# An FNet and gated feed-forward layer on one core: VectorE's extra sums of the last quarter move from ahead of bank Y's drain to behind the sum that frees bank Z

## The chip, the cores and the metric

The kernel runs on one core of a Trainium2 chip. A core has TensorE (PE, matrix products into the banks of PSUM), VectorE (DVE), ScalarE (ACT), GpSimd (POOL) and SyncE (SP, which here issues all the DMAs). Each engine works through its own instructions in the order in which the program lists them and waits on semaphores where it needs another's result. The metric is the device time of one execution in microseconds (us); lower is better.

## The reference

The input is a sequence x of 2048 rows with 448 features in float32. Two sublayers follow each other, each with a layer norm in front and a residual around it:

```python
a = jnp.einsum("bsd,ed->bse", x, dft_hid_re)
b = jnp.einsum("bsd,ed->bse", x, dft_hid_im)
y = jnp.einsum("ts,bse->bte", dft_seq_re, a) - jnp.einsum("ts,bse->bte", dft_seq_im, b)
...
g = jnp.einsum("bsd,df->bsf", x, w_gate)
u = jnp.einsum("bsd,df->bsf", x, w_up)
h = _gelu(g) * u
return jnp.einsum("bsf,fd->bsd", h, w_down)
...
h = x + _A_ref(_layernorm(x, axis=-1), A_dft_seq_re, A_dft_seq_im, A_dft_hid_re, A_dft_hid_im)
h2 = h + _B_ref(_layernorm(h, axis=-1), B_w_gate, B_w_up, B_w_down)
```

The first sublayer is a Fourier mix over features and over the sequence; the second is a gated feed-forward block of width 1792.

## The kernel before

All products run in float16, but each float32 operand is split into a high part (its float16 value, made by ScalarE, line 105) and a low part (what is left, made by VectorE by subtracting the high part, line 109), and three partial products are added. On top of that the products are Strassen-like: sums and differences of blocks are formed first, so that seven block products do the work of eight.

The first half of the span does the Fourier mix and prepares the weights. The second half, which matters here, does the feed-forward block in four **quarters** of 512 rows (by pairs of 256), each of 14 **steps**; a step `t` (0 to 55) computes one block of 128 features of the hidden layer for the quarter's rows. The last quarter is steps 42 to 55. In a step TensorE uses three PSUM banks, X, Y and Z (`GateUp`, from line 1204). Its order in a step of the last three quarters is fixed by the loop from line 1427 on: `x_close`, `z_open` (the first products into Z), eight matmuls of the down projection (`dn_mm`), `y_mid`, ten more of `dn_mm`, `x_open` of the next step, `y_close`, `z_close`, three of `dn_mm`, `y_open` of the next step.

Between them three instructions of VectorE take the results out of the banks:

- the **first Z sum** in `y_mid` (line 1197, `hh<-pZ,u`): the hidden block from Z and from `u3`, ScalarE's copy of Y (line 1245). `z_close` adds more products into Z and so waits for it.
- **Y's drain** in `y_close` (line 1254, `hh<-pY,g`).
- the **second Z sum** in `z_close` (line 1197, `c<-pZ,u`). It frees bank Z: `z_open` of the next step waits for it.

The down projection works on 56 chunks; a chunk takes 128 columns of a quarter's hidden tile, and the blocks of one pair of steps. For each chunk `d` `dn_sums(d)` forms five sums of the hidden blocks (lines 1278 to 1280, into a tile `dn_s` of which there are three) and `dn_split(d)` makes the high and low parts (`dn_w`, or `dn_spare` where a tile no longer needed takes them): two instructions on ScalarE, two on VectorE. In each step `dn_ahead` has the sums of one chunk: GpSimd does the first two instructions, VectorE the last. Their split follows in the next step (the **ordinary split**).

The down projection runs 14 steps behind, so the last quarter's own chunks (numbers 42 to 55) have no step of the loop; TensorE multiplies them in a tail behind step 55. Some of them are therefore summed and split during the last quarter, as soon as their hidden blocks are complete: chunks 42 to 47 in steps 44, 46, 48, 50, 52 and 54, chunks 49 and 50 in steps 45 and 51. All three instructions of these **extra sums** are VectorE's. Their **extra split** follows at the end of the next step.

What stands where is a table `side`: `at(side, (t, k), work)` puts work at place `k` of step `t`, and `do(t, k)` in the loop issues it. Places 0 to 7 stand at given lines of the loop; places 2, 3 and 7 at the end of a step, in this order.

Of the kernel before, what the change touches and what calls it, by code (L numbers as in the profile page):

```python
# [32 lines left out]
def kernel(  # L33
# [38 lines left out]
    V, A, G, PE = nc.vector, nc.scalar, nc.gpsimd, nc.tensor  # L72
# [257 lines left out]
    def x_load(u, parts=(slice(0, 2),)):  # L330
        if parts[0].start == 0:
            t = pair_tile(f"x{u}")
            for g in range(2):
                xt[2 * u + g] = t[:, g, :], t[:, parts[0], :]
        for s in parts:
            src = x_pairs[u][:, s, :]
            t = xt[2 * u + s.start]
            nc.sync.dma_start(t[1] if s.start == 0 else t[0], src if s.start == 0 else src[:, 0, :])
# [9 lines left out]
    def x_stats(*tiles):  # L348
        n, tag = len(tiles), f"x{tiles[0]}"
        mv = norm_x[tiles] = small.tile([P, n, 2], F32, tag=f"mv{n}", name=f"mv_{tag}")  # L350
        sts = [small.tile([P, 6], F32, tag="st", name=f"st_x{i}") for i in tiles]
        for i, st in zip(tiles, sts):
            V.bn_stats(st, xt[i][0])
        for g, st in enumerate(sts):
            V.bn_aggr(mv[:, g, :], st)

    def x_root(*tiles):
        norm_x[tiles] = norm_x[tiles], root(norm_x[tiles], f"x{tiles[0]}")

    def x_rstd_steps(*tiles):  # L360
        mv, sd = norm_x.pop(tiles)
        found = []
        steps = rstd_steps(found, mv, sd, f"x{tiles[0]}")
        next(steps)
        for g, i in enumerate(tiles):
            norm_x[i] = mv, found[0], g
        yield
        yield from steps
# [354 lines left out]
    def at(t, n, *what):  # L723
        t.setdefault(n, []).extend(what)
# [21 lines left out]
    def chain(engine, costs, due, make, after=()):  # L746

        run, last = [], list(after)

        def step(first):  # L750
            if first:
                run.append(make())
            next(run[0])

        for k, cost in enumerate(costs):
            last = [add(engine, cost, due, lambda k=k: step(k == 0), after=last)]
        return last[0]
# [4 lines left out]
    def fixed(n, rank, engine, cost, what, after=(), lag=0.0):  # L762
        if n < FIRST:
            plan(n, rank, what)
            return None
        return add(engine, cost, T[n + 1], what, after=after, begin=T[n] - 1.0, lag=lag)
# [3 lines left out]
    for k, (i, i2) in enumerate(tiles_of):  # L770
        n = where["F", i]
        if k > 2:
            t = fixed(n - 10, 8, "SP", 0.1, lambda u=i // 2: x_load(u), lag=5.0)
            t = fixed(n - 7, 7, "V", 1.35, lambda i=i, j=i2: x_stats(i, j), [t])
            t = fixed(n - 6, 2, "A", 0.3, lambda i=i, j=i2: x_root(i, j), [t])
            if n - 6 < FIRST:
                fixed(n - 6, 5, "V", 0.6, lambda i=i, j=i2: x_rstd(i, j))
            else:
                t = chain("V", (0.2, 0.1, 0.1, 0.1), T[n - 5], lambda i=i, j=i2: x_rstd_steps(i, j), [t])
            t = fixed(n - 6, 5, "V", 0.15, lambda i=i, j=i2: x_bias(i, j), [t])  # L780
        for c in (i, i2):
            n = where["F", c]
# [6 lines left out]
        for c in (i, i2):  # L789
            n = where["F", c]  # L790
# [3 lines left out]
            if is_s(c // 2):  # L794
                t = drained = add("A", 1.05, T[n + 1] + 1.5, lambda i=c: feature_high(i), after=done + ring_w[-2:][:1] * (len(ring_w) > 1))
                t = chain("V", (0.56, 0.36, 0.36), T[n + 2], lambda i=c: feature_sums(i, V), [t])
                t = add("A", 1.45, T[n + 2] + 2.0, lambda i=c: sums_high(i), after=[t])
                t = add("V", 1.7, T[n + 2] + 3.5, lambda i=c: sums_low(i), after=[t])
                ring_w.append(t)
            else:  # L800
                t = add("A", 0.95, T[n + 1] + 1.0, lambda i=c: feature_high(i), after=done)
                t = drained = add("V", 1.07, T[n + 1] + 2.5, lambda i=c: feature_low(i), after=[t])
# [13 lines left out]
    for g, (p, u) in enumerate(units):  # L816
        n = where["U", p, u]
# [14 lines left out]
        if is_s(u):  # L832
            t = chain("V", (0.6, 0.34, 0.34), T[n] - 3.0, lambda p=p, u=u: seq_sums(p, u), [load] + sums_of)
# [11 lines left out]
    for p in range(N_PASS):  # L845
        q, j = divmod(p, 2)
        of_pass = [where["U", p, u] for u in range(N_UNIT)]
        n0, n = min(of_pass), max(of_pass) + 1
# [12 lines left out]
        t = add("A", 0.25, t0 + 14.0, lambda q=q, j=j: ffn_root(q, j), after=m)  # L861
        t = chain("V", (0.2, 0.1, 0.1, 0.1), t0 + 15.0, lambda q=q, j=j: ffn_rstd_steps(q, j), [t])
        last_e, h_done[p] = m, [store, t]
        if q < 2:
            t = add("V", 0.15, t0 + 16.0, lambda q=q, j=j: ffn_bias(q, j), after=[t])
            t = add("A", 1.35, t0 + 17.0, lambda q=q, j=j: ffn_norm_act(q, j, hp[q, j]), after=[t])
            h_done[p] = [store, t]
            for k in range(4):
                t = add("V", 0.36, t0 + 18.0 + k, lambda q=q, j=j, k=k: ffn_sums(q, j, (k,)), after=[t])
            for k in range(2):  # L870
                high = add("A", (0.65, 1.0)[k], t0 + 22.0 + k, lambda q=q, j=j, k=k: ffn_hi(q, j, (k,)), after=[t])
                t = high
            for k in range(5):
                t = add("V", (0.34, 0.87, 0.25, 0.35, 0.25)[k], t0 + 23.0 + k, lambda q=q, j=j, k=k: ffn_lo(q, j, (k,)), after=[t])
# [22 lines left out]
    for k, f in enumerate(order):  # L897
# [5 lines left out]
        t, lows = s2, []  # L903
        for m in range(4):
# [4 lines left out]
            t = high  # L909
# [7 lines left out]
    t = fixed(len(slots) - 14, 9, "SP", 0.1, lambda: down_load(0), last_e, lag=6.0)  # L917
# [349 lines left out]
    NC = NF // 2  # L1267
# [7 lines left out]
    def dn_sums(d, E=G):  # L1275
        t = dn_hid(d)
        s = dn_s[d] = fpool.tile([P, 5, P], F32, tag="dn_s", bufs=DN_S, name=f"dn_s{d}")
        E.tensor_add(s[:, 0:2], t[:, 0:2], t[:, 2:4])
        E.tensor_sub(s[:, 2:4], t[:, 1:4:2], t[:, 0:4:2])  # L1279
        V.tensor_add(s[:, 4], t[:, 0], t[:, 3])  # L1280
# [64 lines left out]
    side = {}  # L1345

    def do(t, k):
        for what in side.pop((t, k), ()):
            what()
# [24 lines left out]

    for n in range(6):
        t = 3 * NF + 2 * n + 2
        at(side, (t, 6), lambda n=n: dn_sums(6 * NC + n, V))
        at(side, (t + 1, 7), lambda n=n: dn_split(6 * NC + n, spare(n, 6 * NC + n) if n < 4 else None))
    for n, t in enumerate((3 * NF + 3, 3 * NF + 9)):
        at(side, (t, 6), lambda n=n: dn_sums(7 * NC + n, V))  # L1380
        at(side, (t + 1, 7), lambda n=n: dn_split(7 * NC + n, spare(4 + n, 7 * NC + n)))

    drains = {}
# [43 lines left out]
    for t in range(N_GU):  # L1427
        q, f = divmod(t, NF)
        if f == 0:
            if q == 1:  # L1430
                quarter0.close()
                odd_q = ctx.enter_context(tc.tile_pool(name="odd_q", bufs=1, side="right"))
            hh[q] = (fpool, odd_q)[q % 2].tile([P, NC, 4, TQ], F32, tag="hh", name=f"hh{q}")
            if 1 <= q <= 2:
                hops_tile(q + 1)
        ahead = {1: 5, 2: 6, 3: 7, 4: 8, 5: 9, 6: 10, 7: 11, 8: 12, 9: 13, 10: 14, 12: 15, 13: 16}.get(t) if t <= NF else t + 2
        if ahead and ahead < N_GU and ahead not in LATE:
            gw_load(ahead)
        d = t - NF
        if d >= 0 and d % NC == 1:  # L1440
            hr_load(d // NC)
        if t in (N_GU - 2, N_GU - 1):
            hr_load(t - N_GU + 8)
        nxt = GateUp(t + 1) if t + 1 < N_GU else None
        if q == 0:
            cur.x_close()
            nxt.x_open()
            if prev:
                prev.c_last()
            cur.y_mid()  # L1450
            late_prep(2 * t)
            if t > 0 and t % 2 == 0 and t < 2 * NC:
                down_hi(t // 2 - 1, 1)
            nxt.z_open()
            nxt.y_open()
            cur.y_close()
            cur.z_close()
            dn_ahead(t)
            if t > 0:
                down_prep(t - 1)  # L1460
            late_prep(2 * t + 1)
        else:
            do(t, 0)
            prev.c_last()
            cur.x_close()
            if t > NF:
                cur.z_open()
            if d + 1 < 6 * NC:
                dn_split(d + 1)
            dn_mm(d, range(0, 8))  # L1470
            cur.y_mid()
            dn_ahead(t)
            do(t, 6)
            dn_mm(d, range(8, 18))
            if nxt:
                nxt.x_open()
            do(t, 1)
            if not nxt:
                dn_mm(d, range(18, 21))
            do(t, 4)  # L1480
            cur.y_close()
            cur.z_close()
            if nxt:
                dn_mm(d, range(18, 21))
            do(t, 5)
            if nxt:
                nxt.y_open()
            if t == 2 * NC:
                down_hi(NC - 1, 1)
            if t == 2 * NC + 1:  # L1490
                down_lo(NC - 1, 1)
            do(t, 2)
            do(t, 3)
            do(t, 7)
        prev, cur = cur, nxt
    A6, A7 = 6 * NC, 7 * NC

# [105 lines left out]
```

## Time and profile before

| | |
|---|---|
| median of 3 runs | 712.17 us (712.1 to 712.65) |
| profiled execution | 712.42 us |
| its span | 710.6 us |
| TensorE busy | 701.3 us (99%) |
| VectorE busy | 544.6 us (77%) |
| ScalarE busy | 399.8 us (56%) |
| GpSimd busy | 197.1 us (28%) |
| granted TensorE clock | 1.0 |

The span is what lies between the first and the last instruction that the profile shows; the execution's time has what lies around it as well. The shares are means over the whole span: the last quarter, from about 590 to 679 us, has its own. In rows of the time line the first number is the start in us from the span's beginning, the second the duration of the group in us; matmuls overlap, so the distance from one group's start to the next tells more than the durations. `x6` is the number of instructions in a group. Buffer numbers are left out: `pZ` is bank Z of any step, `hh` the hidden layer, `hr` the residual rows.

### The profile page before, as it was taken

To read this page: it belongs to the slowest core of one execution; us is meant where nothing else is said; L and a number is where in the kernel's file an instruction comes from. 1 tells how busy PE (TensorE), PEld (TensorE's weight loads), DVE (VectorE), ACT (ScalarE), POOL (GpSimd) and SP (SyncE) were. 2 spreads that over 40 slices of the span, in tenths; PEclk is the share of its full clock that TensorE was granted. 3 is DMA by queue.
4 is the path that set the end of the run, shared out by engine and by line. 5 is a ranking of instruction groups with operands and counts; after the bars stand their busy time and mean duration, and the time that the engine had idled before them with its cause. 6 is when DMAs were issued, how large, how long until landed. Compare 5 with 4: busy or idle time off the path is not lost.

```text
span 710.6 us, 15025 instructions
## 1 busy us (share of the span) xinstructions
PE 701.3 (99%) x5902; PEld 570.6 (80%) x5902; DVE 544.6 (77%) x1131; ACT 399.8 (56%) x845; POOL 197.1 (28%) x225
## 2 busy tenths in 40 slices
PE   7999999999999999999999999999999999999998
PEld 4556567777776868686888889999999999998898
DVE  6799999899988987877368667575765755887876
ACT  5587574757656665645166665555555544454432
POOL 0000000000000000002026664474664745656442
PEclk9999999999999999999999999999999999999999
DMA  9366846799988697758267745847468574445301
GB/s 330 102 151 177 209 155 200 250 206 328 245 221 284 191 245 252 258 162 318 92 238 300 271 172 171 187 165 201 176 196 188 178 208 162 176 156 178 134 28 53
DMA packets 82935, 140.64 MB, mean 198 GB/s; under 512 B 41776, under 2 KB 60464, under 8 KB 82864
## 3 DMA queue, kind: packets, MB, share of 16 engines
q1 hardware_dynamic: 82864, 139.68, 63.8%
q8 instruction: 46, 0.75, 0.4%
q14 instruction: 25, 0.20, 0.1%
HBM read 110.17 MB, written 20.19 MB: 183 GB/s over the span
## 4 chain that ended last, share of the span: by engine, by line
PE 92%; DVE 3%; ACT 2%; issue 1%; DMA 1%; SPq 0%; DVEq 0%; ACTq 0%
PE acc L573 39%; PE acc_d L1132 15%; PE pY L1187 13%; PE pZ L1187 9%; PE ab L456 9%; PE pX L1187 8%; DMA wh_raw<-in_w_hid_dram 1%; DVE dn_w L109 1%; ACT dn_w L105 1%; DVE wh_lo L111 0%; DVE hh L1197 0%; ACT c L1262 0%; DVE dn_s L1280 0%; DVE dn_s L1279 0%; ACT u L1231 0%
## 5 line engine op out<-in xcount | busy, mean ns | idle before, releaser
L1187 PEld LDWEIGHTS <-gw 128*128 128x128 f16 x2184 | 213.3, 98 | 25.4 <-issue 3.0
L573 PE MATMUL acc<-b,ws 128*128 128x448 f16 (+1 forms) x1344 | 221.9, 312 | 0.0
L573 PEld LDWEIGHTS <-ws 128*128 128x128 f16 x1344 | 130.6, 98 | 70.7
L1187 PE MATMUL pY<-hops,gw 128*128 128x256 f16 x952 | 129.1, 273 | 0.0
L1132 PE MATMUL acc_d<-wd,dn_w 128*128 128x224 f16 x1050 | 122.3, 259 | 0.0
L234 POOL TENSOR_TENSOR wd_s<-wd 128x448 f32<-128x448 f32 x7 | 8.4, 1207 | 350.2 <-DMA wr<-in_w_seq_dram 331.7
L1132 PEld LDWEIGHTS <-dn_w 128*128 128x128 f16 x1050 | 101.2, 98 | 2.8
L105 ACT ACTIVATE ws<-wr 128x256 f16<-128x256 f32 (+2 forms) x96 | 63.1, 693 | 61.4 <-PE acc L573 43.5
L573 PE MATMUL acc<-b,wss 128*128 128x224 f16 x768 | 94.5, 259 | 0.0
L1187 PE MATMUL pZ<-hops,gw 128*128 128x256 f16 x616 | 85.5, 272 | 1.9 <-DVE c L1197 1.4
L1264 POOL TENSOR_TENSOR hh<-hh,c 128x256 f32<-128x256 f32 x56 | 45.6, 815 | 145.4 <-ACT c L1262 144.9
L1187 PE MATMUL pX<-hops,gw 128*128 128x256 f16 x616 | 83.3, 273 | 0.0
L111 DVE SCALAR_TENSOR_TENSOR ws<-wr,ws 128x256 f16<-128x256 f32 (+2 forms) x96 | 72.3, 781 | 9.1 <-ACT ws L105 9.0
L573 PEld LDWEIGHTS <-wss 128*128 128x128 f16 x768 | 73.8, 98 | 0.0
L109 DVE TENSOR_TENSOR dn_w<-hh,dn_w 128x256 f16<-128x256 f32 x50 | 25.7, 515 | 50.3 <-ACT dn_w L105 50.0
L456 PEld LDWEIGHTS <-xT 128*128 128x128 f16 x352 | 34.2, 98 | 32.5 <-issue 1.4
L109 DVE TENSOR_TENSOR dn_w<-dn_s,dn_w 128x640 f16<-128x640 f32 x50 | 54.9, 1098 | 7.0 <-ACT dn_w L105 5.9
L1231 ACT ACTIVATE u<-pY 128x256 f32<-128x256 f32 x56 | 21.4, 383 | 61.7 <-PE pY L1187 61.7
L1279 POOL TENSOR_TENSOR dn_s<-hh 128x256 f32<-128x256 f32 x42 | 52.8, 1258 | 0.0
L1226 ACT ACTIVATE pY<-pX 128x256 f32<-128x256 f32 x56 | 20.6, 368 | 50.0 <-PE pX L1187 50.0
L111 DVE SCALAR_TENSOR_TENSOR wss<-wsum,wss 128x1024 f16<-128x1024 f32 x32 | 39.3, 1229 | 9.8 <-ACT wss L105 9.8
L456 PE MATMUL ab<-wh_hi,xT 128*128 128x448 f16 x224 | 45.6, 352 | 0.5 <-DVE wh_hi L435 0.2
(120 smaller groups left out, 906.5 us busy)
## 6 DMA issues: line engine op xcount, KB each, us to landing
gw<-w_dram SPq DMA_DIRECT2D x54, 896.0 KB, 4.9
wr<-in_w_seq_dram SPq DMA_DIRECT2D x64, 512.0 KB, 4.6
gu_raw<-in_w_gu_dram SPq DMA_DIRECT2D x28, 384.0 KB, 4.4
w_dram<-gu_p SPq DMA_DIRECT2D x36, 256.0 KB, 3.0
hx<-in_x_dram SPq DMA_DIRECT2D x8, 448.0 KB, 6.3
h_dram<-hx SPq DMA_DIRECT2D x8, 448.0 KB, 5.3
hr<-h_dram SPq DMA_DIRECT2D x8, 448.0 KB, 5.4
x<-in_x_dram SPq DMA_DIRECT2D x7, 448.0 KB, 6.2
```

What stands on the lines that cost most here:

```text
L105: A.activation(dst, src, AF.Copy, scale=scale)
L109: V.tensor_sub(dst, src, hi)
L111: V.scalar_tensor_tensor(dst, src, scale, hi, op0=ALU.mult, op1=ALU.subtract)
L234: G.tensor_sub(s[:, 2:4], t[:, 0:2], t[:, 2:4])
L456: PE.matmul(feat[i][r][:, :D], xT[i][:, kx, :], w[:, kw, r * D : (r + 1) * D], start=n == 0, stop=n == 10,)
L573: PE.matmul(banks[k][:, cols], lhs, rhs, start=k not in begun, stop=stop, skip_group_check=True)
L1132: PE.matmul(acc[k // 2][:, k % 2 * HD : (k % 2 + 1) * HD], a_of(la, a), b_of(lb, b), start=first and m == 0 and k % 2 == 0, stop=last and ...
L1187: PE.matmul(ps, w[:, wl, wa + ws, :], ops[:, m + ms, :], start=first and n == 0, stop=last and n == len(terms) - 1, skip_group_check=True,)
L1226: A.activation(self.Y, self.X, AF.Copy)
L1231: A.activation(self.u2, self.Y, AF.Copy, scale=SC)
L1264: G.tensor_mul(c22, c22, self.c12)
L1279: E.tensor_sub(s[:, 2:4], t[:, 1:4:2], t[:, 0:4:2])
```

## The change

The extra sums get a place of their own, 8, which stands behind place 7 at the end of a step; place 6, between `y_mid` and `y_close`, goes away. Nothing else is changed. No instruction is added or taken away.

```diff
     for n in range(6):
         t = 3 * NF + 2 * n + 2
-        at(side, (t, 6), lambda n=n: dn_sums(6 * NC + n, V))
+        at(side, (t, 8), lambda n=n: dn_sums(6 * NC + n, V))
         at(side, (t + 1, 7), lambda n=n: dn_split(6 * NC + n, spare(n, 6 * NC + n) if n < 4 else None))
     for n, t in enumerate((3 * NF + 3, 3 * NF + 9)):
-        at(side, (t, 6), lambda n=n: dn_sums(7 * NC + n, V))
+        at(side, (t, 8), lambda n=n: dn_sums(7 * NC + n, V))
         at(side, (t + 1, 7), lambda n=n: dn_split(7 * NC + n, spare(4 + n, 7 * NC + n)))
...
             cur.y_mid()
             dn_ahead(t)
-            do(t, 6)
             dn_mm(d, range(8, 18))
...
             do(t, 7)
+            do(t, 8)
         prev, cur = cur, nxt
```

VectorE in step 44, before, from the ordinary chunk's last sum to the first row of step 45 (`dn_s42` are the extra sums, `pY_44` and `pZ_44` the banks of this step, `dn_w32` the ordinary split):

```order
L1280 TENSOR_TENSOR dn_s32_8173<-hh2_6627 128x128
L1278 TENSOR_TENSOR dn_s42_8177<-hh3_7947 128x256
L1279 TENSOR_TENSOR dn_s42_8177<-hh3_7947 128x256
L1280 TENSOR_TENSOR dn_s42_8177<-hh3_7947 128x128
L1254 SCALAR_TENSOR_TENSOR hh3_7947<-pY_44_8105,g1_44_8142 128x256
L1197 SCALAR_TENSOR_TENSOR c12_44_8211<-pZ_44_8144,u2_44_8129 128x256
L109 TENSOR_TENSOR dn_w32_8244<-hh2_6627,dn_w32_8244 128x256
```

And with the change:

```order
L1280 TENSOR_TENSOR dn_s32_8173<-hh2_6627 128x128
L1254 SCALAR_TENSOR_TENSOR hh3_7947<-pY_44_8105,g1_44_8142 128x256
L1197 SCALAR_TENSOR_TENSOR c12_44_8207<-pZ_44_8144,u2_44_8129 128x256
L1278 TENSOR_TENSOR dn_s42_8222<-hh3_7947 128x256
L1279 TENSOR_TENSOR dn_s42_8222<-hh3_7947 128x256
L1280 TENSOR_TENSOR dn_s42_8222<-hh3_7947 128x128
L109 TENSOR_TENSOR dn_w32_8244<-hh2_6627,dn_w32_8244 128x256
```

The extra sums stand behind the second Z sum (`c12_44`) and directly ahead of the ordinary split. No extra split stands in step 44.

VectorE from the first Z sum of step 45 to that of step 46, before (`dn_s49` are the extra sums of step 45, `dn_spare` the extra split of chunk 42, `dn_w33` the ordinary split):

```order
L1197 SCALAR_TENSOR_TENSOR hh3_7947<-pZ_45_8237,u3_45_8263 128x256
L1280 TENSOR_TENSOR dn_s33_8266<-hh2_6627 128x128
L1278 TENSOR_TENSOR dn_s49_8270<-hh3_7947 128x256
L1279 TENSOR_TENSOR dn_s49_8270<-hh3_7947 128x256
L1280 TENSOR_TENSOR dn_s49_8270<-hh3_7947 128x128
L1254 SCALAR_TENSOR_TENSOR hh3_7947<-pY_45_8198,g1_45_8235 128x256
L1197 SCALAR_TENSOR_TENSOR c12_45_8304<-pZ_45_8237,u2_45_8222 128x256
L109 TENSOR_TENSOR dn_spare_8320<-hh3_7947,dn_spare_8320 128x256
L109 TENSOR_TENSOR dn_spare_8320<-dn_s42_8177,dn_spare_8320 128x640
L109 TENSOR_TENSOR dn_w33_8343<-hh2_6627,dn_w33_8343 128x256
L109 TENSOR_TENSOR dn_w33_8343<-dn_s33_8266,dn_w33_8343 128x640
L1197 SCALAR_TENSOR_TENSOR hh3_7947<-pZ_46_8336,u3_46_8362 128x256
```

And with the change:

```order
L1197 SCALAR_TENSOR_TENSOR hh3_7947<-pZ_45_8237,u3_45_8263 128x256
L1280 TENSOR_TENSOR dn_s33_8266<-hh2_6627 128x128
L1254 SCALAR_TENSOR_TENSOR hh3_7947<-pY_45_8194,g1_45_8235 128x256
L1197 SCALAR_TENSOR_TENSOR c12_45_8300<-pZ_45_8237,u2_45_8218 128x256
L109 TENSOR_TENSOR dn_spare_8316<-hh3_7947,dn_spare_8316 128x256
L109 TENSOR_TENSOR dn_spare_8316<-dn_s42_8222,dn_spare_8316 128x640
L1278 TENSOR_TENSOR dn_s49_8321<-hh3_7947 128x256
L1279 TENSOR_TENSOR dn_s49_8321<-hh3_7947 128x256
L1280 TENSOR_TENSOR dn_s49_8321<-hh3_7947 128x128
L109 TENSOR_TENSOR dn_w33_8343<-hh2_6627,dn_w33_8343 128x256
L109 TENSOR_TENSOR dn_w33_8343<-dn_s33_8266,dn_w33_8343 128x640
L1197 SCALAR_TENSOR_TENSOR hh3_7947<-pZ_46_8336,u3_46_8362 128x256
```

Y's drain and the second Z sum now come directly behind the ordinary sum; the extra sums stand behind the extra split of chunk 42 and ahead of the ordinary split, which is followed by the first Z sum of step 46.

VectorE in step 52 and the start of step 53, before (`dn_s46` are the extra sums, `dn_w50` the extra split, `dn_w40` the ordinary one):

```order
L1197 SCALAR_TENSOR_TENSOR hh3_7947<-pZ_52_8912,u3_52_8938 128x256
L1280 TENSOR_TENSOR dn_s40_8941<-hh2_6627 128x128
L1278 TENSOR_TENSOR dn_s46_8945<-hh3_7947 128x256
L1279 TENSOR_TENSOR dn_s46_8945<-hh3_7947 128x256
L1280 TENSOR_TENSOR dn_s46_8945<-hh3_7947 128x128
L1254 SCALAR_TENSOR_TENSOR hh3_7947<-pY_52_8868,g1_52_8910 128x256
L1197 SCALAR_TENSOR_TENSOR c12_52_8979<-pZ_52_8912,u2_52_8892 128x256
L109 TENSOR_TENSOR dn_w50_8995<-hh3_7947,dn_w50_8995 128x256
L109 TENSOR_TENSOR dn_w50_8995<-dn_s50_8847,dn_w50_8995 128x640
L109 TENSOR_TENSOR dn_w40_9018<-hh2_6627,dn_w40_9018 128x256
L109 TENSOR_TENSOR dn_w40_9018<-dn_s40_8941,dn_w40_9018 128x640
```

And with the change:

```order
L1197 SCALAR_TENSOR_TENSOR hh3_7947<-pZ_52_8912,u3_52_8938 128x256
L1280 TENSOR_TENSOR dn_s40_8941<-hh2_6627 128x128
L1254 SCALAR_TENSOR_TENSOR hh3_7947<-pY_52_8864,g1_52_8910 128x256
L1197 SCALAR_TENSOR_TENSOR c12_52_8975<-pZ_52_8912,u2_52_8888 128x256
L109 TENSOR_TENSOR dn_w50_8991<-hh3_7947,dn_w50_8991 128x256
L109 TENSOR_TENSOR dn_w50_8991<-dn_s50_8897,dn_w50_8991 128x640
L1278 TENSOR_TENSOR dn_s46_8996<-hh3_7947 128x256
L1279 TENSOR_TENSOR dn_s46_8996<-hh3_7947 128x256
L1280 TENSOR_TENSOR dn_s46_8996<-hh3_7947 128x128
L109 TENSOR_TENSOR dn_w40_9018<-hh2_6627,dn_w40_9018 128x256
L109 TENSOR_TENSOR dn_w40_9018<-dn_s40_8941,dn_w40_9018 128x640
```

Here too the extra sums stand between the extra split and the ordinary one.

## The prediction

> **What bounds the kernel now.** I read the page's busy shares first, then the view of who waited for whom, then the time line of the last quarter, which nearly all rows below are from (start, duration, engine, line, operation; in brackets the idle time ahead and who ended it).
>
> ```profile
> PE 701.3 (99%) x5902; PEld 570.6 (80%) x5902; DVE 544.6 (77%) x1131; ACT 399.8 (56%) x845; POOL 197.1 (28%) x225
> PE pZ L1187 <- DVE c L1197: 1.4, 2, 0.7
> ```
>
> TensorE is the bound: any microsecond that is won or lost must show as TensorE waiting or no longer waiting. In all of the span it waits twice for VectorE's second Z sum, `c<-pZ`. How much such waits cost is read from the distance of repeating work, because the ends of matmuls are modelled. In a step, the six matmuls that open the next step's bank X are the mark:
>
> ```profile
> 606.63 0.82 PE L1187 MATMUL pX<-hops,gw 128*128 128x256 f16 x6
> 612.90 0.82 PE L1187 MATMUL pX<-hops,gw 128*128 128x256 f16 x6
> 619.17 0.82 PE L1187 MATMUL pX<-hops,gw 128*128 128x256 f16 x6
> 619.82 0.71 PE L1187 MATMUL pY<-hops,gw 128*128 128x256 f16 x5
> 620.48 0.71 PE L1187 MATMUL pZ<-hops,gw 128*128 128x256 f16 x5
> 625.55 0.82 PE L1187 MATMUL pX<-hops,gw 128*128 128x256 f16 x6
> 644.58 0.82 PE L1187 MATMUL pX<-hops,gw 128*128 128x256 f16 x6
> 648.77 0.82 PE L1187 MATMUL pZ<-hops,gw 128*128 128x256 f16 x6 [0.68 <-DVE c L1197]
> 651.80 0.82 PE L1187 MATMUL pX<-hops,gw 128*128 128x256 f16 x6
> 662.26 0.82 PE L1187 MATMUL pZ<-hops,gw 128*128 128x256 f16 x6 [0.68 <-DVE c L1197]
> 671.56 0.82 PE L1187 MATMUL pX<-hops,gw 128*128 128x256 f16 x6
> ```
>
> The mark at 606.63 stands in step 44, the one at 671.56 in step 54. An undisturbed step takes 612.90 - 606.63 = 6.27. Ten steps from 606.63 to 671.56 take 64.93, so 2.23 us are lost in them. 651.80 - 644.58 = 7.22 is one step with a Z wait: 0.95 too long. The other (at 662.26) has the same idle time, so two of them make 1.90, and the remaining 0.33 is three steps like the one from 619.17 to 625.55, which is 0.11 too long. There the loss is at `z_close`: from 619.82 to 620.48 five matmuls take 0.66, while six of the same shape take 0.65 just before (619.17 to 619.82), so five should take 0.54. I put the same 0.11 inside each 0.95 (`z_close` of steps 50 and 52), which leaves 0.84 for each Z wait. So 1.68 is all that this change can win by freeing bank Z earlier.
>
> **What sits around the place where the sums go.** This is VectorE with its neighbours from the end of step 45 to the middle of step 46:
>
> ```profile
> 615.35 0.41 DVE L1197 SCALAR_TENSOR_TENSOR c<-pZ,u 128x256 f32<-128x256 f32 x1
> 615.79 0.38 ACT L1231 ACTIVATE u<-pY 128x256 f32<-128x256 f32 x1 [1.67 <-PE pY L1187]
> 616.37 0.73 ACT L105 ACTIVATE dn_spare<-dn_s 128x640 f16<-128x640 f32 x1
> 617.13 0.83 DVE L109 TENSOR_TENSOR dn_spare<-dn_s,dn_spare 128x640 f16<-128x640 f32 x1 [0.20 <-ACT dn_spare L105]
> 617.48 1.07 POOL L1264 TENSOR_TENSOR hh<-hh,c 128x256 f32<-128x256 f32 x1 [2.88 <-ACT c L1262]
> 618.02 0.81 DVE L109 TENSOR_TENSOR dn_w<-hh,dn_w 128x256 f16<-128x256 f32 x1
> 618.50 0.38 ACT L1245 ACTIVATE u<-pY 128x256 f32<-128x256 f32 x1
> 618.50 0.91 POOL L1278 TENSOR_TENSOR dn_s<-hh 128x256 f32<-128x256 f32 x1
> 618.75 1.34 DVE L109 TENSOR_TENSOR dn_w<-dn_s,dn_w 128x640 f16<-128x640 f32 x1
> 619.38 1.31 POOL L1279 TENSOR_TENSOR dn_s<-hh 128x256 f32<-128x256 f32 x1
> 620.02 0.41 DVE L1197 SCALAR_TENSOR_TENSOR hh<-pZ,u 128x256 f32<-128x256 f32 x1
> ```
>
> The first Z sum (620.02) had its operand from ScalarE at 618.50 + 0.38 = 618.88, but starts 1.14 later, because VectorE is still in the splits. Its end, 620.43, releases `z_close` at 620.48. So here the low parts of two splits form a chain with no slack: `y_open` of step 46, ScalarE's `u` (615.79), its two high parts, the extra split's low part (617.13 to 617.96), the ordinary split's two low parts, the first Z sum, `z_close`.
>
> **The change part by part.** It moves eight groups of three VectorE instructions (steps 44, 45, 46, 48, 50, 51, 52, 54). It adds and removes none, and no DMA moves; ScalarE, GpSimd and SyncE keep their orders.
>
> *Steps 44, 48, 50, 54: no extra split stands behind the second Z sum.* There the moved sums meet slack:
>
> ```profile
> 609.08 0.41 DVE L1197 SCALAR_TENSOR_TENSOR c<-pZ,u 128x256 f32<-128x256 f32 x1
> 610.84 0.45 DVE L109 TENSOR_TENSOR dn_w<-hh,dn_w 128x256 f16<-128x256 f32 x1 [1.36 <-ACT dn_w L105]
> 637.10 0.47 DVE L109 TENSOR_TENSOR dn_w<-hh,dn_w 128x256 f16<-128x256 f32 x1 [0.45 <-ACT dn_w L105]
> 649.77 0.48 DVE L109 TENSOR_TENSOR dn_w<-hh,dn_w 128x256 f16<-128x256 f32 x1 [1.06 <-ACT dn_w L105]
> 677.55 0.43 DVE L1197 SCALAR_TENSOR_TENSOR hh<-pZ,u 128x256 f32<-128x256 f32 x1 [3.62 <-ACT u L1245]
> ```
>
> In step 44 VectorE idles 1.36 behind the second Z sum, and that sum itself comes earlier once the sums no longer stand ahead of it. In step 48 the same work only changes its place ahead of 637.10, where 0.45 of idle is left; in step 50 1.06 are left behind the sums (649.77), in step 54 3.62. Cost nothing, cover VectorE's wait for ScalarE's high part; without it they would cost at least 0.87 each (below). In step 50 the 0.84 Z wait goes.
>
> *Steps 45, 46, 51, 52: the sums go behind an extra split and ahead of the ordinary one.* By the order of rows they stand between 617.13's instruction and 618.02's. They can't use VectorE's idle time before 617.13, which is a wait of the split ahead of them. Behind them queue the two low parts and the first Z sum, and for this waits `z_close`. In step 52 the other 0.84 goes too. So at `z_close` of steps 46, 47, 52 and 53 the delay grows by X, the time by which the first Z sum is later. What X is, the trace bounds:
>
> ```profile
> 646.06 1.50 POOL L1123 TENSOR_TENSOR hr<-hr,v 128x224 f32<-128x224 f32 x2
> 646.17 0.88 DVE L1278 TENSOR_TENSOR dn_s<-hh 128x256 f32<-128x256 f32 x1
> 646.97 0.88 DVE L1279 TENSOR_TENSOR dn_s<-hh 128x256 f32<-128x256 f32 x1
> 647.97 0.41 DVE L1254 SCALAR_TENSOR_TENSOR hh<-pY,g 128x256 f32<-128x256 f32 x1
> 672.21 0.41 DVE L1278 TENSOR_TENSOR dn_s<-hh 128x256 f32<-128x256 f32 x1
> 673.08 0.41 DVE L1254 SCALAR_TENSOR_TENSOR hh<-pY,g 128x256 f32<-128x256 f32 x1
> 656.39 1.06 POOL L1264 TENSOR_TENSOR hh<-hh,c 128x256 f32<-128x256 f32 x1 [2.82 <-ACT c L1262]
> 657.41 0.90 POOL L1278 TENSOR_TENSOR dn_s<-hh 128x256 f32<-128x256 f32 x1
> 658.28 1.31 POOL L1279 TENSOR_TENSOR dn_s<-hh 128x256 f32<-128x256 f32 x1
> 659.54 1.51 POOL L1123 TENSOR_TENSOR hr<-hr,v 128x224 f32<-128x224 f32 x2
> ```
>
> Alone the three sums take 673.08 - 672.21 = 0.87; beside GpSimd 647.97 - 646.17 = 1.80, where one sum takes 0.88 instead of 0.41: each meeting with a GpSimd instruction costs 0.47. The same is seen at 618.02 (0.81, against 0.45 at 610.84: 0.36 more) and 618.75 (1.34 against 0.83: 0.51 more). Those are two meetings, with GpSimd instructions two and three of a queue of three (617.48, 618.50, 619.38). With the sums in front, the same three GpSimd instructions meet the three sums instead, and the low parts behind them run free: three meetings in place of two. X = 0.87 + 1 x 0.47 = 1.34. Around step 52's start GpSimd has five (656.39 to 659.54, the last row being two), and five VectorE instructions to meet: five in place of two, X = 0.87 + 3 x 0.47 = 2.28. Lower end: no more meetings than before, X = 0.87. Upper end: the sums pay the full 1.80 and the low parts still pay theirs; in the five-deep place 2.28 stays. I take the count of meetings, since it explains each of the rows above.
>
> That the meetings exclude each other is also what the Trainium skill says in "SBUF — State Buffer", section "SBUF: two separate sides": VectorE instructions with two SBUF inputs and GpSimd share a port pair, which one of them holds for a whole instruction while the other blocks, and which isn't a split of bandwidth. The trace agrees (0.88 against 0.41). By that rule the count of meetings decides and the sum is the +4.73 below; if the two instead shared the bandwidth for as long as both have work, the sums would pay their 1.80 everywhere, and the sum would be that of rival C, +6.11.
>
> *The sum.* Won: 2 x 0.84 = 1.68. Lost: 1.34 + 1.34 + 2.28 + 1.34 = 6.30. At `z_close` of step 53 the 0.11 appears anew, which the Z wait had hidden. The other 0.11 stay. -1.68 + 6.30 + 0.11 = +4.73. The tail behind step 55 is TensorE's own, by the last row of the chain that ended last:
>
> ```profile
> 679.37 28.19 PE acc_d L1132 x294
> ```
>
> It only starts later. The profiled span of 710.6 becomes 715.3, its execution 712.42 becomes 717.15; the median shown, 712.17, becomes 716.9.
>
> **The rivals.**
>
> *A. Not slower: the sums keep GpSimd out.* Between 617.96 and 620.02 the low parts need 2.06, of which 0.36 + 0.51 = 0.87 is waiting for GpSimd (that the sums alone also take 0.87 is chance). If five VectorE instructions back to back let GpSimd in only afterwards, the three sums fill exactly those 0.87: X is about 0, and only the win is left, 710.6. It decides if X is below (1.68 - 0.11)/4 = 0.39. For it: 617.13 ran its full 0.83 while GpSimd's 617.48 stretched to 1.07. Against it: at 646.17 and 646.97, back to back, GpSimd got in between.
>
> *B. No extra meeting.* X = 0.87 four times: -1.57 + 3.48 = +1.91, 714.1. For it: GpSimd's third instruction may slip behind the low parts, as 619.38 does now behind 618.75. Against it: it would then meet those, which is a meeting too.
>
> *C. Full price.* 3 x 1.80 + 2.28 - 1.57 = +6.11, 718.3. For it: 1.80 is measured for these very instructions. Against it: only three GpSimd instructions are queued there.
>
> *D. The change doesn't do what it says*, since the two orders keep the same work behind the same waits: then 712.2. Against it: the order shows the sums behind `c<-pZ` in all eight steps.
>
> **How the numbers follow.** Forecast 716.9 with a chance of 0.70, A 0.05, B 0.10, C 0.13, D 0.02. The range 714.1 to 718.3 goes from B to C, the ends of the unknown X. A measurement of this kernel tells about 0.2% (1.4 us) from no change. Slower by more: the forecast, C and nearly all of B, 0.91. Within: D and a part of B in which one of the four places is hidden, 0.05. Faster: A, less a part that lands near no change, 0.04.
>
> **What would show it.** In the changed kernel the waits of `pZ` for `c` are gone, and in their place stand four of `pZ` for `hh L1197`, shown at some 1.2 to 2.3 us each (the one at step 52's `z_close` the longest). The sums in steps 45, 46, 51, 52 last 0.8 to 0.9 and the low parts behind them come down to about 0.45 and 0.83, save in step 52. Steps 44, 48, 50 and 54 are 6.27 to 6.4 long. It would be wrong if the first Z sum in step 46 starts within 0.4 of where it starts now (A), or if GpSimd's queue there is deeper than three.

## The result, and the profile after

The changed kernel takes 717.35 us (median, 717.24 to 718.83), the kernel before 712.19 beside it: 1.0076 times as long, 95% interval 1.0062 to 1.009. A second group of executions, beside 712.34 us of the kernel before, gave 717.8 us and 1.0075 (1.0062 to 1.0087).

In the view of who waited for whom (us in total, times, longest) the row of `pZ` waiting for `c` is gone, and the row of `pZ` waiting for `hh` has grown. Before, it was a single wait of 0.3 us in an earlier quarter (at 425.73), which is still there:

```profile
PE pZ L1187 <- DVE hh L1197: 6.5, 5, 2.3
```

TensorE's time line of the last quarter (start, duration, engine, line, operation) shows the other four of these waits, at `z_close` of steps 46, 47, 52 and 53, and the two marks that answer to 606.63 and 671.56 before:

```profile
606.66 0.82 PE L1187 MATMUL pX<-hops,gw 128*128 128x256 f16 x6
...
619.85 0.71 PE L1187 MATMUL pY<-hops,gw 128*128 128x256 f16 x5
621.92 0.71 PE L1187 MATMUL pZ<-hops,gw 128*128 128x256 f16 x5 [1.36 <-DVE hh L1197]
...
626.98 0.82 PE L1187 MATMUL pX<-hops,gw 128*128 128x256 f16 x6
...
629.70 0.71 PE L1187 MATMUL pZ<-hops,gw 128*128 128x256 f16 x5 [1.36 <-DVE hh L1197]
...
660.73 0.71 PE L1187 MATMUL pY<-hops,gw 128*128 128x256 f16 x5
663.71 1.23 PE L1187 MATMUL pZ<-hops,gw 128*128 128x256 f16 x5 [2.27 <-DVE hh L1197]
...
670.31 0.82 PE L1187 MATMUL pX<-hops,gw 128*128 128x256 f16 x6
670.97 0.71 PE L1187 MATMUL pY<-hops,gw 128*128 128x256 f16 x5
672.91 0.70 PE L1187 MATMUL pZ<-hops,gw 128*128 128x256 f16 x5 [1.24 <-DVE hh L1197]
...
677.98 0.82 PE L1187 MATMUL pX<-hops,gw 128*128 128x256 f16 x6
```

The ten steps take 71.32, so 8.62 us are lost in them, where 2.23 were before. At `z_close` of step 46 the distance 619.85 to 621.92 is 2.07 in place of 0.55, so 1.52 are lost; in step 47 it is 1.52 again, in step 52 2.43, in step 53 1.39. With the two old 0.11 that makes 7.08. The remaining 1.54 come from something else: the five matmuls at 663.71 last 1.23 in place of 0.71, and from there to the next mark it is 6.60, against 5.06 behind the wait in step 46 (621.92 to 626.98). TensorE ran at a lower clock there; this execution took 718.83 us, and the others, at a mean clock of 1.0, took 717.24 to 717.36 with spans of 715.5 to 715.6. So the change itself costs about 5 us, and this one execution 1.5 more.

VectorE and GpSimd from the extra split of step 45 to the first Z sum of step 46, with the change:

```profile
617.16 0.82 DVE L109 TENSOR_TENSOR dn_spare<-dn_s,dn_spare 128x640 f16<-128x640 f32 x1 [0.20 <-ACT dn_spare L105]
617.90 0.95 DVE L1278 TENSOR_TENSOR dn_s<-hh 128x256 f32<-128x256 f32 x1
618.78 0.94 DVE L1279 TENSOR_TENSOR dn_s<-hh 128x256 f32<-128x256 f32 x1
619.65 0.81 DVE L1280 TENSOR_TENSOR dn_s<-hh 128x128 f32<-128x128 f32 x1
620.38 0.41 DVE L109 TENSOR_TENSOR dn_w<-hh,dn_w 128x256 f16<-128x256 f32 x1
620.72 0.81 DVE L109 TENSOR_TENSOR dn_w<-dn_s,dn_w 128x640 f16<-128x640 f32 x1
621.45 0.41 DVE L1197 SCALAR_TENSOR_TENSOR hh<-pZ,u 128x256 f32<-128x256 f32 x1
```

```profile
617.51 1.06 POOL L1264 TENSOR_TENSOR hh<-hh,c 128x256 f32<-128x256 f32 x1 [3.06 <-ACT c L1262]
618.54 0.90 POOL L1278 TENSOR_TENSOR dn_s<-hh 128x256 f32<-128x256 f32 x1
619.40 0.91 POOL L1279 TENSOR_TENSOR dn_s<-hh 128x256 f32<-128x256 f32 x1
```

The two engines take turns: each of the three sums waits for one GpSimd instruction and lasts about 0.53 longer (0.95 for 0.41 alone). Then GpSimd's queue is empty, and the low parts behind run at 0.41 and 0.81, where they took 0.81 and 1.34 before. The first Z sum starts at 621.45, where it started at 620.02; with the 0.03 by which all of this trace is later (606.66 against 606.63) it is 1.40 late.

Around the start of step 52, where GpSimd has five instructions, the sums meet the first three in the same way (0.95, 0.94 and 0.81), and the low parts behind them meet the last two, at 0.88 and 1.27 in place of a bare 0.41 and 0.81:

```profile
661.15 1.50 POOL L1123 TENSOR_TENSOR hr<-hr,v 128x224 f32<-128x224 f32 x2
661.26 0.88 DVE L109 TENSOR_TENSOR dn_w<-hh,dn_w 128x256 f16<-128x256 f32 x1
662.05 1.27 DVE L109 TENSOR_TENSOR dn_w<-dn_s,dn_w 128x640 f16<-128x640 f32 x1
663.25 0.41 DVE L1197 SCALAR_TENSOR_TENSOR hh<-pZ,u 128x256 f32<-128x256 f32 x1
```

### The profile page after: what moved, and what is told of

Its sections match the earlier page's. It is cut to its first block, busy times and chain, and to the rows that moved or that the text cites. A ratio compares the mean times of both kernels' runs of the same rounds, so it can differ in the third digit from the quotient of the medians.

```text
span 717.1 us, 15024 instructions
## 1 busy us (share of the span) xinstructions
PE 702.7 (98%) x5902; PEld 571.3 (80%) x5902; DVE 542.9 (76%) x1131; ACT 399.3 (56%) x845; POOL 194.7 (27%) x225
## 4 chain that ended last, share of the span: by engine, by line
PE 91%; DVE 4%; ACT 2%; issue 1%; DMA 1%; SPq 0%; DVEq 0%; ACTq 0%
PE acc L573 38%; PE acc_d L1132 14%; PE pY L1187 13%; PE pZ L1187 9%; PE ab L456 9%; PE pX L1187 8%; DVE dn_w L109 1%; DMA wh_raw<-in_w_hid_dram 1%; ACT dn_w L105 1%; DVE dn_s L1279 1%; DVE dn_s L1280 0%; DVE hh L1197 0%; DVE wh_lo L111 0%; ACT u L1231 0%; DVE xs L109 0%
## 5 line engine op out<-in xcount | busy, mean ns | idle before, releaser
L109 DVE TENSOR_TENSOR dn_w<-dn_s,dn_w 128x640 f16<-128x640 f32 x50 | 53.2, 1064 | 7.2 <-ACT dn_w L105 6.2
L1279 POOL TENSOR_TENSOR dn_s<-hh 128x256 f32<-128x256 f32 x42 | 51.3, 1220 | 0.0
```

What stands on the lines that cost most here:

```text
L109: V.tensor_sub(dst, src, hi)
```

## The experiments

All times stand beside the kernel before on the same chip: 712.26 us for the first four, 712.34 us for the rest.

**Only the quiet steps.** Against the kernel before:

```diff
-        at(side, (t, 6), lambda n=n: dn_sums(6 * NC + n, V))
+        at(side, (t, 6 if n in (1, 4) else 8), lambda n=n: dn_sums(6 * NC + n, V))
...
+            do(t, 8)
```

> Only the sums of steps 44, 48, 50 and 54 go behind the second Z sum; those of 45, 46, 51 and 52 stay ahead of Y's drain. Theory 1 (the loss is made where an extra split stands ahead of the moved sums, and only there): the Z wait of step 50 goes, 0.84 us, nothing is lost, 711.3 us. Theory 2 (sums ahead of the ordinary split delay the first Z sum wherever they are moved): half of the loss, about 2.4 us slower, 714.6 us.

711.49 us, ratio 0.9995 (0.9986 to 1.0004). The medians are 0.77 apart, as theory 1 has it, but the interval holds no change as well. It excludes theory 2. The marks of its profile say more: the ten steps take 64.10 (607.37 to 671.47) in place of 64.93, 0.83 less where 0.84 was expected. One Z wait is left, that of step 52:

```profile
662.17 0.82 PE L1187 MATMUL pZ<-hops,gw 128*128 128x256 f16 x6 [0.67 <-DVE c L1197]
```

**Only the busy steps.** Of the sums, those of steps 45, 46, 51 and 52 go to place 8, the others stay at place 6.

> Only the sums of steps 45, 46, 51 and 52 are moved, the other four stay. Theory 1: the whole loss of 6.4 us at four z_close and only one Z wait won (0.84 us), so 5.7 us slower than before and 0.8 us slower than the full change, 717.9 us. Theory 2: about 2.4 us slower than before, 714.6 us.

718.75 us, ratio 1.0095 (1.0081 to 1.0108), more than the full change, as only theory 1 has it. TensorE's waits for VectorE in the last quarter are the four of the full change and the Z wait of step 50:

```profile
623.05 0.71 PE L1187 MATMUL pZ<-hops,gw 128*128 128x256 f16 x5 [1.35 <-DVE hh L1197]
630.84 0.71 PE L1187 MATMUL pZ<-hops,gw 128*128 128x256 f16 x5 [1.35 <-DVE hh L1197]
652.74 0.82 PE L1187 MATMUL pZ<-hops,gw 128*128 128x256 f16 x6 [0.68 <-DVE c L1197]
665.68 0.71 PE L1187 MATMUL pZ<-hops,gw 128*128 128x256 f16 x5 [2.28 <-DVE hh L1197]
673.47 0.71 PE L1187 MATMUL pZ<-hops,gw 128*128 128x256 f16 x5 [1.36 <-DVE hh L1197]
```

It is 0.85 above the 717.9 expected. Two of the four executions had a lowered mean clock (0.998); the other two took 718.07 and 718.48. In the profiled one of the two the lowered stretch lies at the very start of the span (9.2 to 12.5 us, at 0.50) where this kernel and the one before do the same work. Its ten steps take 70.74 (607.79 to 678.53), 5.81 more than before, where 5.7 was expected.

**Ahead of the extra split.**

```diff
-            do(t, 7)
             do(t, 8)
+            do(t, 7)
```

> The changed kernel with places 7 and 8 exchanged: the extra sums stand directly behind the second Z sum and ahead of the extra split, in the time in which VectorE idled for 1.24 us waiting for ScalarE. Theory 1: 0.87 us of sums fit into that idle, both Z waits are gone and no z_close is late beyond its 0.11 us: 1.57 us faster than before, 710.6 us. If the gain of the two Z waits isn't real (bank Z is not what TensorE really waits for): 712.2 us. If the sums are late for the first Z sum in any case: 714 us or more.

710.67 us, ratio 0.998 (0.997 to 0.999): faster than the kernel before, and the 1.59 between the medians is the expected 1.57. By the marks of its profile the ten steps take 63.39 (607.61 to 671.00), 1.54 less. No wait of TensorE for `c` or `hh` is left in the last quarter (two of 0.3 us for `hh` stand in earlier ones). VectorE at the end of step 45:

```profile
615.83 0.42 DVE L1197 SCALAR_TENSOR_TENSOR c<-pZ,u 128x256 f32<-128x256 f32 x1
616.17 0.42 DVE L1278 TENSOR_TENSOR dn_s<-hh 128x256 f32<-128x256 f32 x1
616.50 0.42 DVE L1279 TENSOR_TENSOR dn_s<-hh 128x256 f32<-128x256 f32 x1
616.84 0.28 DVE L1280 TENSOR_TENSOR dn_s<-hh 128x128 f32<-128x128 f32 x1
617.49 0.42 DVE L109 TENSOR_TENSOR dn_spare<-hh,dn_spare 128x256 f16<-128x256 f32 x1 [0.37 <-ACT dn_spare L105]
```

The sums fill time in which VectorE waits for ScalarE anyway, and GpSimd is not at work yet, so each takes its bare 0.42 and 0.28. The same three instructions, two places earlier in VectorE's queue, cost nothing; a Z wait that is taken away is won whole.

**GpSimd's sums a step ahead.**

```diff
-            dn_ahead(t)
+            if t <= 3 * NF:
+                dn_ahead(t)
...
+            if t >= 3 * NF and nxt:
+                dn_ahead(t + 1)
             do(t, 2)
...
-    DN_S = 3
+    DN_S = 4
```

> The changed kernel, but from step 43 on GpSimd forms the ordinary chunk's sums at the end of the step before (with a fourth dn_s tile), so that beside the moved sums it has one instruction left in place of three (five). Theory 1 (each meeting with a GpSimd instruction costs 0.47 us): X falls from 1.4 (2.3) to about 0.4, so 1.7 us for four z_close against 1.7 won: 712.0 us. Rival (the sums' own length and the place are what costs, GpSimd doesn't matter): 717.3 us as the changed kernel.

716.26 us, ratio 1.0061 (1.0047 to 1.0075): neither. The edit didn't do what its expectation said. GpSimd's queue runs ahead of the steps, and the sums, a step earlier in the program, still came right behind the instruction that meets the first moved sum. Three waits stayed (1.35, 1.35, 2.27). Only the sums of step 52 had a single GpSimd instruction beside them, because no ordinary sums are left to follow it. There they last 0.95, 0.41 and 0.28, so only the one that meets GpSimd is long, and the wait in step 53 is gone. TensorE's clock is lowered just before it in this profile, which can take that wait away by itself (see the last run). But the three executions at a mean clock of 1.0 took 716.0 to 716.26, about 1.1 less than those of the changed kernel in the first group, which fits two meetings less at one place. This is a hint for theory 1; the next run is the test.

**Less of GpSimd beside the sums.**

```diff
-        if NF <= t < 6 * NC + 12:
+        if NF <= t < 6 * NC + 12 and t != 46:
             dn_sums(t - 12)
+        if t == 44:
+            dn_sums(34)
...
-            at(side, (t0 + 1 + n, 3), lambda p=p, n=n: drains[p].sums((2 * n, 2 * n + 1)))
+            at(side, (t0 + 1 + (2 if p == 4 and n == 3 else n), 3), lambda p=p, n=n: drains[p].sums((2 * n, 2 * n + 1)))
```

> The changed kernel with two pieces of GpSimd's work taken out of the way: the ordinary sums of step 46 are formed in step 44 (into a tile that is free then), and the last two residual sums of the fifth drain one step earlier. Beside the moved sums of step 45 GpSimd then has one instruction in place of three, beside those of step 51 three in place of five; at steps 46 and 52 nothing changes. Theory 1 (0.47 us per meeting): the wait of z_close in step 46 shrinks by about 0.95, in step 52 by about 0.95, those of steps 47 and 53 stay: 1.9 us faster than the changed kernel, 715.4 us. Rival (GpSimd doesn't matter): 717.3 us, and four waits as in the changed kernel.

715.26 us, ratio 1.0041 (1.0027 to 1.0055). TensorE's waits in the last quarter, and VectorE's sums of step 45 (the edit shifts their line numbers by three):

```profile
620.32 0.71 PE L1187 MATMUL pZ<-hops,gw 128*128 128x256 f16 x5 [0.29 <-DVE hh L1197]
628.11 0.71 PE L1187 MATMUL pZ<-hops,gw 128*128 128x256 f16 x5 [1.35 <-DVE hh L1197]
661.20 0.71 PE L1187 MATMUL pZ<-hops,gw 128*128 128x256 f16 x5 [1.36 <-DVE hh L1197]
668.98 0.71 PE L1187 MATMUL pZ<-hops,gw 128*128 128x256 f16 x5 [1.35 <-DVE hh L1197]
```

```profile
617.37 0.95 DVE L1281 TENSOR_TENSOR dn_s<-hh 128x256 f32<-128x256 f32 x1
618.25 0.41 DVE L1282 TENSOR_TENSOR dn_s<-hh 128x256 f32<-128x256 f32 x1
618.58 0.28 DVE L1283 TENSOR_TENSOR dn_s<-hh 128x128 f32<-128x128 f32 x1
```

The wait in step 46 falls from 1.36 to 0.29, that in step 52 from 2.27 to 1.36, and the two that weren't touched stay. At each of the two places two meetings less are worth 1.07 and 0.91, so about half a microsecond for each meeting. Only the sum that meets GpSimd's one remaining instruction is long. The rival, that GpSimd doesn't matter, falls.

**The sums twice.** The three instructions of `dn_sums` are issued a second time for chunks 43, 46, 49 and 50.

> The changed kernel with the extra sums of steps 45, 46, 51 and 52 formed twice in a row (the second time the same values into the same tile; the output doesn't change). Theory 1 (VectorE's row of instructions from the extra split to the first Z sum has no slack, and all of GpSimd's queue is met by then): 0.87 us more at each of four z_close, 3.5 us more than the changed kernel, 720.8 us. Rival (the place has some slack that the first group used up only in part, or the wait is not VectorE's length): less than 2 us more. The waits of TensorE then reach about 2.4 to 3.3 us; if such waits lower the granted clock, as in the profiled execution of the changed kernel behind its 2.3 us wait, each costs up to 1.4 us more.

723.1 us, ratio 1.0149 (1.0135 to 1.0163). In step 45 the second group is not met by GpSimd and the first Z sum starts at 622.28 where it was 621.45. With the 0.05 by which this trace is earlier (606.61 against 606.66) it is 0.88 later, and TensorE's wait grows as much (1.36 to 2.23):

```profile
619.60 0.81 DVE L1280 TENSOR_TENSOR dn_s<-hh 128x128 f32<-128x128 f32 x1
620.34 0.41 DVE L1282 TENSOR_TENSOR dn_s<-hh 128x256 f32<-128x256 f32 x1
...
622.28 0.41 DVE L1197 SCALAR_TENSOR_TENSOR hh<-pZ,u 128x256 f32<-128x256 f32 x1
```

So there is no slack at this place. The waits in steps 47 and 52 grow alike, to 2.23 and 3.15. The total is 2.3 above the 720.8 of this alone, and most of that is the clock's: all four executions had a mean clock of 0.995 to 0.997, and the profile shows it lowered behind the second and the third wait. Step 46 takes 8.66 by the marks (619.15 to 627.81), step 47 with the same wait 10.25 (to 638.06), 1.59 more. Step 52 takes 11.25 (663.24 to 674.49), 1.68 more than the 6.27 + 2.43 + 0.87 of an undisturbed step with its losses. In step 53 the wait shrinks to 0.98 in return, and the step takes 7.41, 1.25 less than step 46. Together that is 2.0.

**The change again.**

> The changed kernel itself, for the chip of this group and for more executions: 717.3 us. If the lower clock behind the longest wait of TensorE is a matter of chance, some of the executions stand about 1.4 us above the others.

717.8 us (717.26 to 718.34); this is the second group named in the result. Two of the five executions had a lowered mean clock (0.997 and 0.998). In the profiled one of them the clock fell behind the wait of step 52 again, but no step of 1.4 shows: the profiled one took 717.54, less than two at full clock. Its time line says why:

```profile
663.66 0.71 PE L1187 MATMUL pZ<-hops,gw 128*128 128x256 f16 x5 [2.27 <-DVE hh L1197]
664.49 0.97 PE L1187 MATMUL pY<-hops,gw 128*128 128x256 f16 x6
665.26 1.27 PE L1187 MATMUL pX<-hops,gw 128*128 128x256 f16 x5
...
670.39 0.82 PE L1187 MATMUL pX<-hops,gw 128*128 128x256 f16 x6
671.05 0.71 PE L1187 MATMUL pY<-hops,gw 128*128 128x256 f16 x5
671.60 0.70 PE L1187 MATMUL pZ<-hops,gw 128*128 128x256 f16 x5
```

From the wait's end to the next mark it is 6.73 in place of 5.06, 1.67 lost to the clock. But here the clock fell only when `y_open` (664.49) was more than half through; ScalarE and VectorE went on at their own pace, and when TensorE came to `z_close` of step 53, the first Z sum was there: 671.05 to 671.60 is 0.55, the 1.39 to 1.52 of that wait are gone. In the first profile the clock fell ahead of `y_open`, ScalarE's `u` came late too, and both losses stood.

## Why the prediction was right

- **What bounds the kernel, and the win.** Right: both Z waits were real, and worth what the distance of the marks gave. Exchanging the two places won 1.59 us between the medians and 1.54 by the marks for the expected 1.57.
- **The quiet steps cost nothing.** Right: in steps 44, 48, 50 and 54 no new wait appears, and moving only these is no slower.
- **The busy steps lose at the next `z_close`.** Right in place and number: four waits, at steps 46, 47, 52 and 53, the one in step 52 the longest. Moving only these four groups gives the whole loss and more.
- **X by counting meetings.** Right: the three sums met GpSimd's three instructions and the low parts behind ran free; in step 52 there were five meetings, as counted. The price of a meeting was a little small: 0.47, taken from the sums of step 50, where the sums here paid 0.53. X came out at about 1.41 in steps 46 and 47 (1.52 less the 0.11) and 2.32 in step 52 (2.43 less 0.11), where 1.34 and 2.28 stood. With 0.53 for the sums' extra meeting, 0.87 + 0.53 = 1.40; with 0.47 and 0.46 for the two low parts that meet GpSimd in step 52, 0.87 + 0.53 + 0.47 + 0.46 = 2.33. In step 53 of the first profile X was 1.28, behind the lowered clock; in the run of the busy steps alone that wait is 1.36 like those of steps 46 and 47.
- **One reading was wrong.** The two meetings before were with GpSimd's first and second instruction, not its second and third: the low part at 618.02 comes up while GpSimd's 617.48 still runs (to 618.55), the one at 618.75 while 618.50 does (to 619.41), and 619.38 is the one that then waits for VectorE. The count of two, on which X rests, stays.
- **The sum.** +4.73 forecast, +5.16 between the medians, about +4.9 between the spans of executions at full clock (715.5 against 710.6). The term that was short is X, by 0.04 to 0.07 at each place; with 1.41 three times and 2.32 once the same sum gives +4.98.
- **The rivals.** A (the sums keep GpSimd out) was wrong: the engines took turns. B (X = 0.87) and C (X = 1.80) both miss the measured 1.41, and against C the low parts behind the sums ran at their bare 0.41 and 0.81. D fell with the four waits.
- **The clock.** The prediction has no term for a lowered clock. That the medians came out so near is in part luck: six of the nine executions of the changed kernel had a mean clock of 1.0, and in one more a shorter wait took the loss back. The first profiled execution, at 718.83, lies above the range, and so does, by little, one at 718.34.

The lock that the Trainium skill describes in "SBUF — State Buffer", section "SBUF: two separate sides", agrees with the rows of steps 45 and 46: one VectorE sum and one GpSimd instruction alternate (617.90, 618.54, 618.78, 619.40, 619.65), and the one that comes second is delayed, while a Z sum with its operand in PSUM keeps its 0.41 beside GpSimd (620.02 before, beside GpSimd's 619.38 to 620.69).

## What to carry to other kernels

Before moving work to the end of a step, look at what stands between it and the next instruction that another engine waits for: VectorE's idle time ahead of a waiting instruction is of use only to work that is queued ahead of that instruction. Here three instructions cost 1.4 to 2.3 us at each place behind the extra split and nothing ahead of it. When work moves on an engine that takes turns with another, count the other's queued instructions in the new place, not only the durations at the old one.

## What the runs showed of the hardware

In several profiles TensorE's granted clock fell behind its longest wait. In the first profile of the changed kernel the stretches ahead of, at and behind that wait read (busy time and count by engine, granted clock, share of the DMA engines, GB/s):

```profile
655.00:663.00 8.00, 6.44 (x62) 5.83 (x60) 6.24 (x9) 3.49 (x10) 4.59 (x6) 1.00 0.34 115
663.00:667.20 4.20, 3.49 (x19) 2.54 (x19) 1.62 (x5) 0.39 (x2) 0.00 (x0) 0.59 0.58 176
667.20:675.00 7.80, 6.56 (x64) 5.94 (x62) 6.09 (x11) 3.56 (x10) 2.80 (x3) 1.00 0.50 202
```

Over 4.2 us at the end of a wait shown as 2.27 us and behind it the clock was 0.59; in finer stretches it is 0.50 for about 3.4 us, from 663.5 to 666.9. In this execution that cost 1.54 us, about a third of what the change itself costs; in the profile of the change run again a like fall cost next to nothing, since it took the place of a wait for VectorE. The profiles taken together hold seven TensorE waits for VectorE of 2.23 to 3.15 us in the last quarter. Behind five of them the clock is 0.50 for about 3.4 us; behind the 2.28 of the busy steps alone and the first 2.23 of the sums formed twice it stays 1.0. Behind none of the fourteen waits of 0.98 to 1.36 us did it fall.

That the wait lowers the clock is the likely reading, but it isn't shown by a run made for it. In the profile of the busy steps alone the clock falls at 9.2 us, far from these waits, and single executions of kernels without any such wait have a mean clock of 0.998 or less too: two of 21 of the kernel before beside the first four runs, two of 11 of the quiet steps alone, one of 11 with the sums ahead of the extra split. A mean clock without a profile doesn't say where it was lowered. The Trainium skill ("TensorE: Matmul & The Clock Gate", section "Part 1: The HAM clock gate") puts the lower clock behind an idle window of about 3.4 us; here it stood behind waits of 2.2 to 2.3 us in four profiles. So a stall of this length on TensorE may cost more than its own length.
